# Opening stage of a fused attention, rational MLP and PReLU MLP kernel: zero products ahead of the first scores, two-bank scores, other staging of the loads, and earlier places for three readers of finished accumulators

## The chip, the cores and the metric

One core of one Trainium2 chip. The metric is the device time of one execution in microseconds. The kernel before took 1590.13 us (median of 3 runs, 1588.19 to 1590.34).

## What is computed

Three layers in a row on 2 sequences of 3008 rows, all in float32:

```python
scores = (1/3008) * z @ z.T                 # z: 2 x 3008 x 64
x = u * (maximum(scores, 0)**2 @ v)         # u, v: 2 x 3008 x 256
h = x @ w_in                                # 256 -> 2048
P = a0 + a1*h + a2*h**2 + a3*h**3
Q = 1 + |b0|*|h| + |b1|*h**2
x = (P / (Q + 1e-6)) @ w_out                # 2048 -> 256
h = x @ w_in2                               # 256 -> 2048
out = (maximum(h, 0) + alpha*minimum(h, 0)) @ w_out2
```

The weights of both MLPs are float64 and reach the chip as pairs of 32-bit words; the kernel decodes them itself.

## The kernel before, in words

**Tiling.** The rows are cut into 12 blocks (b, j) of 512 (the last of a sequence has 448). A product of float32 operands is made of float32r products of high and low parts, so a block has 190 attention matmuls (48 of scores, 142 of values), 192 of the first MLP and 192 of the second: 574, and 6888 for the 12 blocks, each of 128x128 by 512 columns (or 448).

**Attention.** `a_stream` walks the blocks; a step takes one pair of key tiles, kp of 12. `a_scores` makes two score tiles with two matmuls each (L266, L267), from zA and zB, which hold high and low parts of z. Relu by ScalarE (L268, one for each of the two tiles), then Square (L269), then `split` into ahi (L91 on ScalarE; for block (0, 0) L93 on VectorE) and alo (L94 on VectorE). `a_values` adds the step's product with vt three steps later (LAG_A) to the accumulator acca (L297, L306). After the last step `a_end` multiplies acca by u (L336, tile ut) and stores the block to DRAM. There is one accumulator acca, shared in PSUM (tag acc0) with the second MLP's acc2; acc1 has the first MLP's.

**Opening.** The first HEAD=30 attention steps run alone. Beside them the sixteen pieces of the first MLP's weights are loaded (`words`, L148, on SyncE's queue), decoded (`decode`: L133, L136, L139, L141, L142, L143 on VectorE and L134 on ScalarE) and split (L93, L94 on VectorE). `weights_due` says how many pieces are due by a step: RD0=0.62 per step. In the first 12 steps z (L213, L218, L225) and v (L100, L91, L93, L94) of the first sequence are loaded and split as well. All these loads, and ut, share the two buffers of the tag "raw" (RAW=2). The tag "big" has 28 buffers: 12 of vt and 16 of weights.

**Then** 40 steps of the first MLP (`m1_hidden`, `m1_back`, 24 matmuls each) are spread over the other 115 attention steps, and the second MLP's weights are decoded and spilled to DRAM (`spill_w`, every fifth step, except steps 64 to 75). Then the rest of the first MLP runs against the second. `m1_end` (L424) and `m2_end` (L462) copy finished accumulators out by ScalarE.

**Order.** Each engine has one queue, in order. A scheduler writes the order before the run: of what is ready by its own clock, what comes first in the program goes first. `tc.high_priority(EARLY)` counts an instruction as 100 places earlier. Constants (the four a, the two b, alpha, and sg and sal made from alpha: L187 to L201) are made at the start.

Of the kernel before, what the change touches and what calls it, by code (L numbers as in the profile page):

```python
# [7 lines left out]
F32 = mybir.dt.float32  # L8
# [12 lines left out]

HEAD, X1 = 30, 40

RD0, RD = 0.62, 0.62

# [4 lines left out]
EARLY = 100  # L30
# [5 lines left out]
def relu2_attention_rational_mlp_prelu_mlp(  # L36
# [47 lines left out]

    def raw_tile(nm):
        return tmp.tile([P, 1024], F32, tag="raw", name=nm, bufs=RAW)


# [23 lines left out]
    def load_v(b, kp):  # L112

        raw = raw_tile("vraw")
        r3 = raw.rearrange("p (c d) -> p c d", c=4)
        r0 = kp * 2 * P
        load_rows(r3, v[b], r0, min(S - r0, 4 * P))
        for i in range(2):
            t = big.tile([P, 2, 2, D], F32R, tag="big", name="vt")
            split(t[:, 0], t[:, 1], r3[:, 2 * i : 2 * i + 2, :], on_act=b > 0 or i % 2 == 0)  # L120
            if kp + i == NKP - 1:

                h2 = t[HALF:P, 0, 1].bitcast(F32)
                nc.vector.tensor_tensor(t[HALF:P, 1, 1], h2, h2, ALU.subtract)
            vt[b, kp + i] = t
# [20 lines left out]
    def words(src):  # L146
        raw = tmp.tile([P, 2, 512], I32, tag="raw", name="wraw", bufs=RAW)
        nc.sync.dma_start(out=raw, in_=src.rearrange("(c p) f -> p c f", p=P))  # L148
        return raw.rearrange("p c (n t) -> p (c n) t", t=2)
# [31 lines left out]
    def fill_w(store, jp):  # L181
        t = late.get("w", big).tile([P, 2, 2, 256], F32R, tag="big", name="w")
        nc.gpsimd.dma_start(out=t.rearrange("p k c d -> p k (c d)"), in_=store[jp])
        store[jp] = t

    sc = const.tile([P, 8], F32, name="sc")
    nc.gpsimd.dma_start(out=sc[:, 0:4], in_=pa[None, :].to_broadcast([P, 4]))  # L187
    nc.gpsimd.dma_start(out=sc[:, 4:6], in_=pb[None, :].to_broadcast([P, 2]))
    cb = const.tile([P, 2], F32, name="cb")
    nc.scalar.activation(cb, sc[:, 4:6], AF.Abs)  # L190
    one = const.tile([P, 1], F32, name="one")
    ONE = 1.0 + 1e-6
    nc.vector.memset(one, ONE)
    al = const.tile([P, NF], F32, name="al")
    nc.gpsimd.dma_start(out=al, in_=alpha.rearrange("(c p) -> p c", p=P))

    sg = const.tile([P, NF], F32, name="sg")
    nc.vector.tensor_scalar(sg, al, 1.0, -2.0, ALU.is_gt, ALU.mult)
    nc.vector.tensor_scalar(sg, sg, 1.0, None, ALU.add)
    sal = const.tile([P, NF], F32, name="sal")  # L200
    nc.vector.tensor_tensor(sal, al, sg, ALU.mult)  # L201
    a0, a1, a2, a3 = (sc[:, i : i + 1] for i in range(4))
# [6 lines left out]
    def load_z(b, g):  # L209

        raw = raw_tile("zraw")
        n = qn[g]
        nc.sync.dma_start(out=raw[:, 0:n], in_=zt[b, :, g * QB : g * QB + n])  # L213
        if n % P:
            nc.sync.dma_start(out=raw[:, n : n + HALF], in_=zt[b, :, S - HALF : S])
            n += HALF
        t = zp.tile([P, QB], F32R, tag="z", name="zA")
        nc.vector.tensor_copy(t[:, 0:n], raw[:, 0:n])  # L218
        if (b, g) == (0, 0):
            zB[b, g] = zp.tile([P, QB], F32R, tag="z", name="zB")  # L220
            nc.scalar.copy(zB[b, g][HALF:P, 0:n], raw[HALF:P, 0:n])
            nc.vector.tensor_tensor(
                zB[b, g][0:HALF, 0:n], raw[0:HALF, 0:n], t[0:HALF, 0:n].bitcast(F32), ALU.subtract
            )
        nc.vector.tensor_tensor(  # L225
            t[HALF:P, 0:n], raw[HALF:P, 0:n], t[HALF:P, 0:n].bitcast(F32), ALU.subtract
        )
        zA[b, g] = t
# [24 lines left out]
    def a_scores(b, j, kp):  # L253
        n = qn[j]
        r = tmp.tile([P, 2, QB], F32, tag="t", name="r", bufs=TT)
        pair = None
        if not x1 and kp % 2:
            pair = psw.tile([P, 2, QB], F32, tag="h", name="sp")
        for i in range(2):
# [7 lines left out]
            nc.tensor.matmul(s, w, zB[b, j][:, :n], start=False, stop=True)  # L267
            nc.scalar.activation(r[:, i, :n], s, AF.Relu, scale=1.0 / S)  # L268
        nc.scalar.activation(r[:, :, :n], r[:, :, :n], AF.Square)  # L269
        hi = hlp.tile([P, 2, QB], F32R, tag="hl", name="ahi")  # L270
        lo = hlp.tile([P, 2, QB], F32R, tag="hl", name="alo")
        on_act = (b, j) != (0, 0)
        if kp < NKP - 1:
            split(hi[:, :, :n], lo[:, :, :n], r[:, :, :n], on_act)
        else:

            if on_act:
                nc.scalar.copy(hi[:, :, :n], r[:, :, :n])
            else:
                nc.vector.tensor_copy(hi[:, :, :n], r[:, :, :n])  # L280
            for dst, rows, i in ((lo, slice(0, P), 0), (hi, slice(HALF, P), 1)):
# [51 lines left out]
    def a_end(b, j):  # L333
        n = qn[j]
        t = uts.pop((b, j))
        nc.vector.tensor_tensor(t[:, :, :n], acc_a[b, j][:, :, :n], t[:, :, :n], ALU.mult)  # L336
        xd[b, j] = dr.tile([P, ND, QB], F32, name=f"xd{b}_{j}")
# [80 lines left out]
    def m1_end(q):  # L418
# [4 lines left out]
        t = tmp.tile([P, ND, QB], F32, tag="raw", name="x2", bufs=RAW)  # L423
        nc.scalar.copy(t[:, :, :n], acc1[q][:, :, :n])  # L424
        x2d[q] = dr.tile([P, ND, QB], F32, name=f"x2d{q[0]}_{q[1]}")
# [32 lines left out]
    def m2_end(q):  # L458
        b, j = q
        n = qn[j]  # L460
        t = tmp.tile([P, ND, QB], F32, tag="raw", name="ot", bufs=RAW)
        nc.scalar.copy(t[:, :, :n], acc2[q][:, :, :n])  # L462
        r0 = b * S + j * QB
# [156 lines left out]
```

## Time and profile before

| | |
|---|---|
| median of 3 runs | 1590.13 us |
| profiled execution, its own time | 1588.01 us |
| its span, first to last instruction | 1586.2 us |
| TensorE matmul | 1555.5 us busy, 6888 instructions |
| VectorE (DVE) | 1405.0 us busy, 1505 instructions |
| ScalarE (ACT) | 1183.9 us busy, 1473 instructions |
| GpSimd (POOL) | 28.1 us busy, 55 instructions |
| mean granted clock of TensorE | 0.998 |

A busy time is the union of the spans in which an engine has an instruction in flight; matmuls overlap, so a matmul's own duration (0.39 us) is longer than the distance to the next one, and the distance is what a matmul costs. The same holds for VectorE and ScalarE in a lesser degree. x counts the instructions that touch a stretch, so one that is cut by its edge counts on both sides. The name in brackets behind an instruction of the timeline is how long its engine had been idle before it, and what ended that. PE is TensorE, PEld its weight load, SPq and POOLq the queues of SyncE and GpSimd.

### The profile page before, as it was taken

What the parts mean: (1) busy time and instruction counts of PE and PEld (TensorE: products, weight loads), DVE (VectorE), ACT (ScalarE), POOL (GpSimd) and SP (SyncE); (2) the same over time, 40 slices, a digit from 0 to 9 for tenths busy, and PEclk for the clock granted to TensorE, in tenths of its full rate; (3) what the DMA queues carried; (4) which work ended last, traced back from release to release, by engine and by line L of the source; (5) the groups of instructions that cost most, each with busy time, mean ns of one, the idle gap of its engine ahead of it and who ended that gap; (6) DMA issues with size and microseconds to landing.
All of it is one profiled execution on the core that took longest, in us unless ns stands there. A gap on an engine that the chain in (4) does not pass through costs nothing.

```text
span 1586.2 us, 18045 instructions
## 1 busy us (share of the span) xinstructions
PE 1555.5 (98%) x6888; PEld 1288.9 (81%) x6888; DVE 1405.0 (89%) x1505; ACT 1183.9 (75%) x1473; POOL 28.1 (2%) x55
## 2 busy tenths in 40 slices
PE   7799999999999999999999999999999999999998
PEld 5587788788888888888888888888888888888888
DVE  7998989999899899877999989899899999898963
ACT  5598899989988899988576666676666666676643
POOL 0000000000000000001000000000000000000000
PEclk9999999999999999999999999999999999999999
DMA  4433211233212121104301000100101000000000
GB/s 126 132 100 120 61 52 54 80 97 93 61 53 87 42 84 41 58 34 149 127 1 40 26 27 1 41 27 25 41 0 39 14 27 35 17 14 27 14 1 25
DMA packets 39911, 83.03 MB, mean 52 GB/s; under 512 B 3600, under 2 KB 12816, under 8 KB 39824
## 3 DMA queue, kind: packets, MB, share of 16 engines
q1 hardware_dynamic: 32800, 65.09, 12.8%
q0 software_dynamic: 7024, 16.79, 3.4%
q8 instruction: 54, 0.88, 0.2%
q14 instruction: 33, 0.27, 0.1%
HBM read 52.64 MB, written 26.41 MB: 50 GB/s over the span
## 4 chain that ended last, share of the span: by engine, by line
PE 89%; DVE 5%; ACT 3%; DMA 1%; issue 1%; POOL 0%; DVEq 0%; SPq 0%; ACTq 0%; POOLq 0%
PE acc L297 21%; PE acca L297 13%; PE h L288 11%; PE h L289 10%; PE acc L306 10%; PE h L290 10%; PE acca L306 6%; PE s L266 3%; PE s L267 3%; DVE alo L94 1%; ACT r L269 1%; ACT r L268 1%; ACT ahi L91 0%; DMA zraw<-in_z_dram 0%; DVE ahi L93 0%
## 5 line engine op out<-in xcount | busy, mean ns | idle before, releaser
L297 PE MATMUL acc<-ghi,w 128*128 128x512 f32 (+1 forms) x1536 | 377.7, 385 | 0.0
L297 PEld LDWEIGHTS acc<-ghi,w 128*128 128x128 f32 x1536 | 288.2, 188 | 54.0 <-ACT ghi L91 0.2
L297 PE MATMUL acca<-ahi,vt 128*128 128x512 f32 (+1 forms) x1152 | 292.6, 389 | 7.5 <-DVE ut L336 5.5
L288 PE MATMUL h<-xhi,w 128*128 128x512 f32 (+1 forms) x768 | 296.5, 387 | 0.1
L289 PE MATMUL h<-xlo,w 128*128 128x512 f32 (+1 forms) x768 | 296.2, 386 | 0.0
L290 PE MATMUL h<-xhi,w 128*128 128x512 f32 (+1 forms) x768 | 296.0, 386 | 0.0
L297 PEld LDWEIGHTS acca<-ahi,vt 128*128 128x128 f32 x1152 | 216.8, 189 | 53.1 <-DVE ut L336 6.7
L392 ACT ACTIVATE sq<-h 128x1024 f32<-128x1024 f32 (+1 forms) x96 | 97.3, 1013 | 154.2 <-PE h L290 147.9
L443 ACT ACTIVATE m<-h,sal 128x512 f32<-128x512 f32 (+1 forms) x192 | 127.8, 680 | 106.7 <-PE h L290 106.1
L306 PE MATMUL acc<-glo,w 128*128 128x512 f32 (+1 forms) x768 | 203.5, 385 | 0.3 <-DVE glo L409 0.3
L94 DVE TENSOR_TENSOR alo<-r,ahi 128x1024 fp32r<-128x1024 f32 (+1 forms) x132 | 158.1, 1199 | 36.0 <-PE acc L297 18.5
L288 PEld LDWEIGHTS h<-xhi,w 128*128 128x128 f32 x768 | 144.2, 188 | 30.5 <-DVE m L444 0.9
L94 DVE TENSOR_TENSOR glo<-m,ghi 128x1024 fp32r<-128x1024 f32 (+1 forms) x96 | 115.2, 1200 | 58.7 <-PE acc L297 41.9
L289 PEld LDWEIGHTS h<-xlo,w 128*128 128x128 f32 x768 | 144.2, 188 | 27.4 <-DVE xlo L94 0.7
L306 PEld LDWEIGHTS acc<-glo,w 128*128 128x128 f32 x768 | 144.1, 188 | 27.5 <-DVE glo L409 0.7
L290 PEld LDWEIGHTS h<-xhi,w 128*128 128x128 f32 x768 | 144.2, 188 | 26.9
L268 ACT ACTIVATE r<-s 128x512 f32<-128x512 f32 (+1 forms) x256 | 143.6, 598 | 26.2 <-DVE t L408 20.3
L306 PE MATMUL acca<-alo,vt 128*128 128x512 f32 (+1 forms) x552 | 150.6, 389 | 2.6 <-DVE alo L94 2.6
L444 DVE SCALAR_TENSOR_TENSOR m<-h,sg,m 128x512 f32<-128x512 f32 (+1 forms) x192 | 138.6, 736 | 16.2 <-ACT m L443 15.5
L269 ACT ACTIVATE r<-r 128x1024 f32<-128x1024 f32 (+1 forms) x144 | 151.8, 1058 | 1.6
L396 DVE SCALAR_TENSOR_TENSOR ab<-sq,cb,ab 128x1024 f32<-128x1024 f32 (+1 forms) x96 | 120.7, 1258 | 14.3 <-ACT ab L393 14.1
L406 DVE SCALAR_TENSOR_TENSOR ghi<-t,sc,sq 128x1024 fp32r<-128x1024 f32 (+1 forms) x96 | 120.9, 1259 | 10.8 <-ACT sq L402 5.6
(70 smaller groups left out, 2083.1 us busy)
## 6 DMA issues: line engine op xcount, KB each, us to landing
wraw<-in_moe_w_in_dram SPq DMA_DIRECT2D x16, 512.0 KB, 3.7
wraw<-in_moe_w_out_dram SPq DMA_DIRECT2D x16, 512.0 KB, 3.6
wd<-dec POOLq DMA_DIRECT2D x32, 256.0 KB, 2.3
w<-wd POOLq DMA_DIRECT2D x16, 512.0 KB, 4.2
vraw<-in_v_dram SPq DMA_DIRECT2D x10, 512.0 KB, 3.8
ut<-in_u_dram SPq DMA_DIRECT2D x10, 512.0 KB, 3.7
xd<-ut SPq DMA_DIRECT2D x10, 512.0 KB, 2.6
xr<-xd SPq DMA_DIRECT2D x10, 512.0 KB, 3.3
```

Of the source, the lines that this page charges most:

```text
L94: nc.vector.tensor_tensor(dst_lo, src, dst_hi.bitcast(F32), ALU.subtract)
L268: nc.scalar.activation(r[:, i, :n], s, AF.Relu, scale=1.0 / S)
L269: nc.scalar.activation(r[:, :, :n], r[:, :, :n], AF.Square)
L288: nc.tensor.matmul(acc, w_hi, hi, start=first, stop=False)
L289: nc.tensor.matmul(acc, w_hi, lo, start=False, stop=False)
L290: nc.tensor.matmul(acc, w_lo, hi, start=False, stop=last)
L297: nc.tensor.matmul(acc[:, e, :n], w[:, k, i, e * P : (e + 1) * P], hi[:, i, :n], start=first and i == 0 and k == 0, stop=False,)
L306: nc.tensor.matmul(acc[:, e, :n], w[:, 0, i, e * P : (e + 1) * P], lo[:, i, :n], start=False, stop=last and i == both - 1,)
L396: nc.vector.scalar_tensor_tensor(ab, sq, b1, ab, ALU.mult, ALU.add)
L406: nc.vector.scalar_tensor_tensor(hi, t, a0, sq, ALU.add, ALU.mult)
L443: nc.scalar.activation(t[:, i], h, AF.Copy, scale=sal[:, f : f + 1])
L444: nc.vector.scalar_tensor_tensor(t[:, i], h, sg[:, f : f + 1], t[:, i], ALU.mult, ALU.max)
```

## The change

The first 36 attention steps run alone (30 before), with RD0 0.4 and RD 0.55 pieces of weights per step. Nine matmuls of a zeroed tile (WARM) stand ahead of everything. In the opening the scores of a step lie in two neighbouring banks, in turn of tag h and of the still unused acc1, and one Relu reads both. Block (0, 0) splits on ScalarE like the others. The first sequence's z and v are staged in buffers of the tag "big". The weight words come by GpSimd's queue. Constants are made on GpSimd, with alpha laid out by the host, loaded first. zA's low part is made ahead of zB. The readers of finished accumulators count as 100 places earlier.

```diff
@@ -19,9 +19,11 @@
 
 LAG_A, LAG_M = 3, 2
 
-HEAD, X1 = 30, 40
-
-RD0, RD = 0.62, 0.62
+HEAD, X1 = 36, 40
+
+RD0, RD = 0.4, 0.55
+
+WARM = 9
 
 SP, AV0, AV1 = 5, 64, 76
 
@@ -82,8 +84,18 @@
     zp = zctx.enter_context(tc.tile_pool(name="zp", bufs=ZP))
     late = {}
 
-    def raw_tile(nm):
+    def raw_tile(nm, early=False):
+
+        if early:
+            return big.tile([P, 1024], F32, tag="big", name=nm)
         return tmp.tile([P, 1024], F32, tag="raw", name=nm, bufs=RAW)
+
+
+    wz = hlp.tile([P, QB], F32R, tag="hl", name="wz")
+    nc.vector.memset(wz.bitcast(F32), 0.0)
+    wps = psw.tile([P, QB], F32, tag="s", bufs=2, name="wps")
+    for i in range(WARM):
+        nc.tensor.matmul(wps, wz[:, 0:P], wz, start=i == 0, stop=i == WARM - 1)
 
 
     def split(dst_hi, dst_lo, src, on_act=True):
@@ -111,7 +123,7 @@
 
     def load_v(b, kp):
 
-        raw = raw_tile("vraw")
+        raw = raw_tile("vraw", b == 0)
         r3 = raw.rearrange("p (c d) -> p c d", c=4)
         r0 = kp * 2 * P
         load_rows(r3, v[b], r0, min(S - r0, 4 * P))
@@ -145,7 +157,7 @@
 
     def words(src):
         raw = tmp.tile([P, 2, 512], I32, tag="raw", name="wraw", bufs=RAW)
-        nc.sync.dma_start(out=raw, in_=src.rearrange("(c p) f -> p c f", p=P))
+        nc.gpsimd.dma_start(out=raw, in_=src.rearrange("(c p) f -> p c f", p=P))
         return raw.rearrange("p c (n t) -> p (c n) t", t=2)
 
     def raw_w(src, jp, wide):
@@ -183,22 +195,26 @@
         nc.gpsimd.dma_start(out=t.rearrange("p k c d -> p k (c d)"), in_=store[jp])
         store[jp] = t
 
+    al = const.tile([P, NF], F32, name="al")
+    nc.gpsimd.dma_start(out=al, in_=alpha)
     sc = const.tile([P, 8], F32, name="sc")
     nc.gpsimd.dma_start(out=sc[:, 0:4], in_=pa[None, :].to_broadcast([P, 4]))
     nc.gpsimd.dma_start(out=sc[:, 4:6], in_=pb[None, :].to_broadcast([P, 2]))
     cb = const.tile([P, 2], F32, name="cb")
-    nc.scalar.activation(cb, sc[:, 4:6], AF.Abs)
     one = const.tile([P, 1], F32, name="one")
     ONE = 1.0 + 1e-6
     nc.vector.memset(one, ONE)
-    al = const.tile([P, NF], F32, name="al")
-    nc.gpsimd.dma_start(out=al, in_=alpha.rearrange("(c p) -> p c", p=P))
 
     sg = const.tile([P, NF], F32, name="sg")
-    nc.vector.tensor_scalar(sg, al, 1.0, -2.0, ALU.is_gt, ALU.mult)
-    nc.vector.tensor_scalar(sg, sg, 1.0, None, ALU.add)
     sal = const.tile([P, NF], F32, name="sal")
-    nc.vector.tensor_tensor(sal, al, sg, ALU.mult)
+
+    nc.gpsimd.tensor_scalar(sg, al, 1.0, -2.0, ALU.is_gt, ALU.mult)
+    nc.gpsimd.tensor_scalar(sg, sg, 1.0, None, ALU.add)
+    nc.gpsimd.tensor_tensor(sal, al, sg, ALU.mult)
+    nc.gpsimd.tensor_scalar(cb, sc[:, 4:6], 0.0, 2.0, ALU.is_ge, ALU.mult)
+    nc.gpsimd.tensor_scalar(cb, cb, -1.0, None, ALU.add)
+    nc.gpsimd.tensor_tensor(cb, sc[:, 4:6], cb, ALU.mult)
+
     a0, a1, a2, a3 = (sc[:, i : i + 1] for i in range(4))
     b0, b1 = cb[:, 0:1], cb[:, 1:2]
 
@@ -208,7 +224,7 @@
 
     def load_z(b, g):
 
-        raw = raw_tile("zraw")
+        raw = raw_tile("zraw", b == 0)
         n = qn[g]
         nc.sync.dma_start(out=raw[:, 0:n], in_=zt[b, :, g * QB : g * QB + n])
         if n % P:
@@ -216,15 +232,15 @@
             n += HALF
         t = zp.tile([P, QB], F32R, tag="z", name="zA")
         nc.vector.tensor_copy(t[:, 0:n], raw[:, 0:n])
+        nc.vector.tensor_tensor(
+            t[HALF:P, 0:n], raw[HALF:P, 0:n], t[HALF:P, 0:n].bitcast(F32), ALU.subtract
+        )
         if (b, g) == (0, 0):
             zB[b, g] = zp.tile([P, QB], F32R, tag="z", name="zB")
             nc.scalar.copy(zB[b, g][HALF:P, 0:n], raw[HALF:P, 0:n])
             nc.vector.tensor_tensor(
                 zB[b, g][0:HALF, 0:n], raw[0:HALF, 0:n], t[0:HALF, 0:n].bitcast(F32), ALU.subtract
             )
-        nc.vector.tensor_tensor(
-            t[HALF:P, 0:n], raw[HALF:P, 0:n], t[HALF:P, 0:n].bitcast(F32), ALU.subtract
-        )
         zA[b, g] = t
 
 
@@ -253,9 +269,13 @@
     def a_scores(b, j, kp):
         n = qn[j]
         r = tmp.tile([P, 2, QB], F32, tag="t", name="r", bufs=TT)
+
         pair = None
-        if not x1 and kp % 2:
-            pair = psw.tile([P, 2, QB], F32, tag="h", name="sp")
+        if not x1:
+            if kp % 2:
+                pair = psw.tile([P, 2, QB], F32, tag="h", name="sp")
+            else:
+                pair = psa.tile([P, 2, QB], F32, tag="acc1", name="sq")
         for i in range(2):
             k = 2 * kp + i
             w = zA[b, k // 4][:, (k % 4) * P : (k % 4 + 1) * P]
@@ -265,19 +285,18 @@
                 s = psw.tile([P, QB], F32, tag="s", bufs=2, name="s")[:, :n]
             nc.tensor.matmul(s, w, zA[b, j][:, :n], start=True, stop=False)
             nc.tensor.matmul(s, w, zB[b, j][:, :n], start=False, stop=True)
-            nc.scalar.activation(r[:, i, :n], s, AF.Relu, scale=1.0 / S)
+            if pair is None:
+                nc.scalar.activation(r[:, i, :n], s, AF.Relu, scale=1.0 / S)
+        if pair is not None:
+            nc.scalar.activation(r[:, :, :n], pair[:, :, :n], AF.Relu, scale=1.0 / S)
         nc.scalar.activation(r[:, :, :n], r[:, :, :n], AF.Square)
         hi = hlp.tile([P, 2, QB], F32R, tag="hl", name="ahi")
         lo = hlp.tile([P, 2, QB], F32R, tag="hl", name="alo")
-        on_act = (b, j) != (0, 0)
         if kp < NKP - 1:
-            split(hi[:, :, :n], lo[:, :, :n], r[:, :, :n], on_act)
+            split(hi[:, :, :n], lo[:, :, :n], r[:, :, :n])
         else:
 
-            if on_act:
-                nc.scalar.copy(hi[:, :, :n], r[:, :, :n])
-            else:
-                nc.vector.tensor_copy(hi[:, :, :n], r[:, :, :n])
+            nc.scalar.copy(hi[:, :, :n], r[:, :, :n])
             for dst, rows, i in ((lo, slice(0, P), 0), (hi, slice(HALF, P), 1)):
                 nc.vector.tensor_tensor(
                     dst[rows, i, :n], r[rows, i, :n], hi[rows, i, :n].bitcast(F32), ALU.subtract
@@ -333,7 +352,8 @@
     def a_end(b, j):
         n = qn[j]
         t = uts.pop((b, j))
-        nc.vector.tensor_tensor(t[:, :, :n], acc_a[b, j][:, :, :n], t[:, :, :n], ALU.mult)
+        with tc.high_priority(EARLY):
+            nc.vector.tensor_tensor(t[:, :, :n], acc_a[b, j][:, :, :n], t[:, :, :n], ALU.mult)
         xd[b, j] = dr.tile([P, ND, QB], F32, name=f"xd{b}_{j}")
         nc.sync.dma_start(out=xd[b, j][:, :, :n], in_=t[:, :, :n])
 
@@ -421,7 +441,8 @@
             x2[q] = split_x(acc1[q], n)
             return
         t = tmp.tile([P, ND, QB], F32, tag="raw", name="x2", bufs=RAW)
-        nc.scalar.copy(t[:, :, :n], acc1[q][:, :, :n])
+        with tc.high_priority(EARLY):
+            nc.scalar.copy(t[:, :, :n], acc1[q][:, :, :n])
         x2d[q] = dr.tile([P, ND, QB], F32, name=f"x2d{q[0]}_{q[1]}")
         nc.sync.dma_start(out=x2d[q][:, :, :n], in_=t[:, :, :n])
 
@@ -459,7 +480,8 @@
         b, j = q
         n = qn[j]
         t = tmp.tile([P, ND, QB], F32, tag="raw", name="ot", bufs=RAW)
-        nc.scalar.copy(t[:, :, :n], acc2[q][:, :, :n])
+        with tc.high_priority(EARLY):
+            nc.scalar.copy(t[:, :, :n], acc2[q][:, :, :n])
         r0 = b * S + j * QB
         nc.sync.dma_start(
             out=out[:, r0 : r0 + n].rearrange("(e p) s -> p e s", p=P), in_=t[:, :, :n]
@@ -602,6 +624,8 @@
             a = a.transpose(0, 2, 1)
         if name == "z":
             a = _np.concatenate([a, a], axis=2).transpose(0, 2, 1)
+        if name == "moe2_alpha":
+            a = a.reshape(-1, 128).T
         a = _np.ascontiguousarray(a)
         if a.dtype == _np.float64:
             a = a.view(_np.int64)
```

## Rows read from the trace of the kernel before

**Rows 1.** The page: busy times, and tenths of each of 40 slices.
```profile
PE 1555.5 (98%) x6888; PEld 1288.9 (81%) x6888; DVE 1405.0 (89%) x1505; ACT 1183.9 (75%) x1473; POOL 28.1 (2%) x55
...
PE   7799999999999999999999999999999999999998
```

**Rows 2.** Windows: PE, PEld, DVE, ACT, POOL busy (x), granted clock, DMA share, GB/s.
```profile
0.00:160.00 160.00, 136.22 (x547) 104.34 (x548) 140.11 (x228) 112.44 (x160) 3.67 (x9) 0.98 0.40 119
40.00:80.00 40.00, 29.92 (x108) 20.70 (x107) 37.88 (x64) 22.55 (x33) 0.00 (x0) 0.92 0.46 132
80.00:120.00 40.00, 40.00 (x174) 32.30 (x173) 37.36 (x66) 36.56 (x51) 0.00 (x0) 0.99 0.33 99
120.00:160.00 40.00, 36.65 (x158) 28.52 (x157) 34.92 (x52) 32.97 (x45) 1.10 (x2) 1.00 0.38 118
160.00:300.00 140.00, 140.00 (x613) 113.53 (x612) 128.20 (x136) 128.12 (x162) 5.32 (x10) 1.00 0.19 59
```

**Rows 3.** Chain that ended last, one steady step of 24 matmuls: start, us, what.
```profile
1058.76 1.81 PE acc L297 x8
...
1064.20 1.81 PE acc L297 x8
```

**Rows 4.** Timeline, the start on VectorE and TensorE: start, us, engine, line.
```profile
0.81 0.06 DVE L193 MEMSET one<- 128x1 f32 x1 [0.81 <-PEq L597]
3.51 0.43 DVE L218 CAST zA<-zraw 128x512 fp32r<-128x512 f32 x1 [2.65 <-DMA zraw<-in_z_dram]
7.45 0.17 DVE L198 TENSOR_SCALAR sg<-al 128x16 f32<-128x16 f32 x1 [2.79 <-DMA al<-in_moe_alpha_dram]
7.66 0.69 DVE L225 TENSOR_TENSOR zA<-zraw,zA 64x512 fp32r<-64x512 f32 x1
8.40 0.80 PE L266 MATMUL s<-zA 128*128 128x512 f32 x1 [8.40 <-DVE zA L225]
...
15.00 1.26 PE L297 MATMUL acca<-ahi,vt 128*128 128x512 f32 x3
16.10 0.40 PE L266 MATMUL sp<-zA 128*128 128x512 f32 x1
```

**Rows 5.** Waits of TensorE over the span: us in total, times, longest.
```profile
PE s L266 <- DVE zA L225: 9.3, 2, 8.4
PE acca L297 <- DVE ut L336: 5.5, 2, 3.2
```

**Rows 6.** Waits of ScalarE, 0 to 150 us.
```profile
ACT dec L134 <- DVE dec L133: 24.5, 7, 4.9
```

**Rows 7.** Timeline of VectorE, 45 to 48 us: the distances between starts.
```profile
45.53 0.68 DVE L143 TENSOR_TENSOR dec<-dec 128x512 f32<-128x512 f32 x1
46.13 1.22 DVE L94 TENSOR_TENSOR alo<-r,ahi 128x1024 fp32r<-128x1024 f32 x1
47.27 0.42 DVE L93 CAST w<-dec 128x512 fp32r<-128x512 f32 x1
47.61 0.42 DVE L133 TENSOR_SCALAR dec<-wraw 128x512 f32<-128x512 f32 x1
```

**Rows 8.** Timeline of ScalarE: Relu, Square and ahi, two each without idle time.
```profile
21.16 1.08 ACT L268 ACTIVATE r<-s 128x512 f32<-128x512 f32 x2
72.24 2.01 ACT L269 ACTIVATE r<-r 128x1024 f32<-128x1024 f32 x2
74.14 2.00 ACT L91 CAST ahi<-r 128x1024 fp32r<-128x1024 f32 x2
```

**Rows 9.** The page: a two-bank read of PSUM by ScalarE.
```profile
L392 ACT ACTIVATE sq<-h 128x1024 f32<-128x1024 f32 (+1 forms) x96 | 97.3, 1013 | 154.2 <-PE h L290 147.9
```

**Rows 10.** The page: DMA issues, KB each, median us to landing.
```profile
wraw<-in_moe_w_in_dram SPq DMA_DIRECT2D x16, 512.0 KB, 3.7
...
w<-wd POOLq DMA_DIRECT2D x16, 512.0 KB, 4.2
```

**Rows 11.** The instructions of line L288: ns min/median/max, first and last start.
```profile
L288 PE MATMUL h<-xhi,w x768: 362/389/501, 145.4 to 1573.3; 128*128 128x512 f32 x160, 128*128 128x448 f32 x32
```

## The prediction

> **What bounds the kernel now.** I read the page first. TensorE is busy in nearly every slice [rows 1], so the question is where it issues more slowly than it can. A steady first-MLP step shows the pace: 24 matmuls in 1064.20 - 1058.76 = 5.44 us, so 0.2267 us each [rows 3]. The windows are then read by their matmul counts, not by their busy times. Up to 160 us there are 547 matmuls; at that pace they need 124.0 us, so **36.0 us are lost in the opening**. From 160 to 300 us 613 matmuls need 139.0 of 140 us: behind the opening little is lost [rows 2]. Of the 36.0 us, 8.4 go before the first matmul [rows 4]. 40 to 80 us holds 108 matmuls where 176 would fit, some 15.5 us lost; 80 to 120 us holds 174 and loses next to nothing; 120 to 160 us holds 158 and loses 4 [rows 2].
>
> Next, why. VectorE is busy for 37.88 of the 40 us from 40 to 80 us, and ScalarE for only 22.55 [rows 2]: VectorE is the bound there; the granted clock is 0.92, as TensorE waits. ScalarE stood still behind it, 24.5 us at the second step of the weight decode [rows 6]. TensorE's waits name the rest: 9.3 us for zA, of which 8.4 are the start, and 5.5 us for the product with u, which sits in the same VectorE queue [rows 5]. At the start zA's second half (L225) runs at 7.66 us although z was there at 3.51 us, because sg (L198), ahead of it in the queue, waited for alpha [rows 4].
>
> **The needs of the opening, in us, before and after.** Distances between starts are what an instruction costs: on VectorE 0.60 for L143, 1.14 for alo, 0.34 for a 512-wide cast [rows 7]. One piece of weights is three passes like L133 and one cast (0.34 each) and four like L143 (0.60): 3.76. Ahi on VectorE is taken as 0.60 too.
>
> - VectorE, 30 steps before: alo 30 x 1.14 = 34.2; ahi of block (0, 0) 12 x 0.60 = 7.2; 16 pieces 60.2; v, twelve low parts and seven casts, 9.6; z 6.2; u 2.3. Sum 119.7. TensorE needs 30 x 15.83 x 0.2267 = 107.7. VectorE is 12.0 over.
> - VectorE, 36 steps after: alo 41.0; ahi moves to ScalarE; 60.2; 9.6; 6.2; u 3.4. Sum 120.4, against 36 x 15.83 x 0.2267 = 129.2 on TensorE: 93%. Up to step 12, where z and v are still being split, 4 pieces in place of 6 make it 44.5 against 43.1, so it is no longer far behind there either.
> - ScalarE after: one two-bank Relu, bounded by half of L269's pair (1.0) and by a two-bank read of PSUM, 1.01 [rows 8, 9]; with Square 1.0 and ahi 1.0 [rows 8] that is 3.0 per step, 108 for 36; v casts and decode passes, 22 at about 0.54 (half of L268's pair), 12. Sum 120: 93%. The two single Relus cost 1.08 before, so merging saves 0.07 a step and no more; the move of ahi adds 12 x 1.0.
>
> So the six extra steps and the slower weights give TensorE more to do while VectorE's pile is worked off, and no engine is over-booked. **What the opening then loses:**
>
> 1. The start. The memset of the zero tile costs between 0.06 (a 128x1 memset) [rows 4] and 0.42 (a cast of its size) [rows 7] behind 0.81 us. Nine matmuls at the start's spacing follow. Before, 15 matmuls ran from 8.40 to 16.10 us with one wait of about 1 us in them; I take 0.43 each, which is the lower of the clock's two levels, 1.2 GHz for 512 columns. They end at 4.8 to 5.1 us. The constants now wait on POOL, so zA is complete at about 3.51 + 0.34 + 0.60, with some latency 4.7. First real matmul at **5.1** in place of 8.4.
> 2. The clock. Those 15 matmuls lost 15 x 0.2 = 3.0 us; spacing came down at 16.10, 7.7 us after TensorE's first matmul [rows 4]. The nine zero products take 3.8 of that. Between nothing and 1.9 us remains: **1.0**. That zero products raise the clock is shown by no row; if they don't, it is the 3.0 again.
> 3. Filling. Scores, Relu, Square, ahi come one after another, about 4 us, before the first values; steps 2 and 3 need the second z. Twelve early loads no longer wait for two buffers (12 loads, 12 vt and the 4 pieces of weights due by step 12 are just the 28 buffers of "big"), but they share the wires. 0 to 4; I take **2.0**.
> 4. The rest of some 125 us. Like 160 to 300 us, with both engines at about 92%, it would lose 0.7%, 0.9 us; like 120 to 160 us 10%, 12.5. Loads by engine put it near the first, the uneven decode work near the second: **7.0**.
>
> Together 15.1 in place of 36.0: **20.9 gained**. The 5.5 us of the waits for u are inside the 36.0 and not counted again; an earlier place helps only the product that is ready. No wait of TensorE names the two ScalarE copies L424 and L462, so their new places gain nothing; each moves one 1.0 us instruction past its neighbours, cost nothing while ScalarE has a tenth of its time free (128.12 of 140 us) [rows 2].
>
> **Given back.** 40 first-MLP steps go on 109 attention steps, not 115: 0.367 per step for 0.348. With seven two-bank VectorE passes of 1.14 or more, that adds 0.15 us to VectorE's 5.02 (128.20/140 of 5.48) [rows 2] while the step grows to 5.59: 93% for 92%. The spills begin ten steps later and end at step 130, five before the fills. 0 to 3 us; I take **1.5**.
>
> The weight words pass from SP's queue to POOL's. On POOL the median from issue to landing is 4.2 us for such a size, on SP 3.7 [rows 10]. 0.5 us each is hidden by two buffers and a decode every 1.8 to 2.5 steps (6 us or more); were it not, 16 x 0.5 = 8 us would fill VectorE's slack of 8.8 in the opening and no more. Between 0 and 8 I take 0. Behind a late load stands all of VectorE's work behind L133. On SP's queue the loads of z, v and u stand behind 16 issues fewer in the opening; on POOL's, the spills' stores come only after step 40. The Trainium skill speaks against this move ("SBUF — State Buffer", section "SBUF: two separate sides"): descriptors of POOL's loads can't be written while VectorE holds the shared port in certain passes, and the load then seems blocked by VectorE; the SP queue is free of that. By [rows 10] the sum stays as it is; by that rule it would be the third rival below.
>
> **Sum:** 1588.0 (the profiled execution: span 1586.2 and 1.8 around it) - 20.9 + 1.5 = 1568.6. The median of the runs is 2.1 above the profiled execution; I go between and say **1570**.
>
> **Rivals.**
>
> - *All of it comes in* (0.15). Items 2 and 3 at nothing, item 4 as from 160 to 300 us: 5.1 + 0.9 lost, 30 gained, 1.5 given back: 1559.5. For it: nothing is over-booked. Against: a static order written for other durations.
> - *ScalarE takes VectorE's place* (0.20). It now has ahi, and stays in order behind decodes: with the 24.5 us of [rows 6] unchanged its need is 144.5 against 129.2, 15 in place of the 7 of item 4; with the 5.5 for u as well the loss is 28.9, the gain 7.1 - 1.5: 1582. For it: 93% booked. Against: the wait follows VectorE's lateness, which shrinks.
> - *Late weight words* (0.05). If each load holds VectorE at L133 for 1.5 us, three times the difference of [rows 10], that is 16 x 1.5 = 24 us, less the slack of 8.8: 15 more, 1585. It decides from 8.8/16 = 0.55 us per load. Against: each load has a whole decode's time to land.
> - *The middle jams*, **slower** (0.07). Place: attention beside the first MLP, about 600 us. Price: where VectorE was 95% booked and late, TensorE lost 15.5 of 40 us [rows 2]. It decides from 100% of 5.59 us on VectorE; 93% is reckoned. If a tenth of that stretch fell into it, 60 x 0.39 = 23 us more: 1592. Against: 80 to 120 us was at 93% and lost nothing.
> - *The change doesn't do what it says* in one part, the zero products: 2 us, within the forecast's own range.
>
> The forecast itself has 0.53, its own range 1563 to 1577. A measurement of this kernel can tell 0.2%, 3.2 us, from no change. Faster takes the forecast, the first rival, and most of the next two, 0.88; same 0.05, slower 0.07. The range reaches over most of the first rival and into the second: 1559 to 1582.
>
> **What would show it.** First score matmul near 5 us, at 0.23 us spacing before 10; 40 to 80 us with 160 matmuls or more; VectorE and ScalarE both near 93% there; no wait for ut above 1 us; ScalarE's wait for L133 well under 24.5; the first h matmul of the first MLP at 142 to 150 us, where it was (145.4) [rows 11], yet six steps further; windows behind 300 us as before. Wrong: under 150 matmuls from 40 to 80 us, VectorE waiting for weight words, or matmul counts behind 160 us down by more than 1%.

## The result, and the profile after

The changed kernel takes **1570.13 us** (median of 4 runs, 1568.46 to 1571.51) against 1590.18 us for the kernel before (here 4 runs, where the prediction had 3): a ratio of 0.9876, 95% interval 0.9859 to 0.9893. That is 20.0 us less. The forecast was 1570, with a range from 1559 to 1582.

The page of the changed kernel, busy times and TensorE's slices:

```profile
PE 1551.7 (99%) x6897; PEld 1291.1 (82%) x6897; DVE 1399.4 (89%) x1491; ACT 1191.8 (76%) x1445; POOL 54.2 (3%) x93
...
PE   8999999999999999999999999999999999999998
```

The windows answer to [rows 2]; columns as there:

```profile
0.00:160.00 160.00, 150.80 (x636) 121.42 (x637) 138.03 (x212) 133.59 (x151) 18.23 (x31) 0.99 0.39 120
...
40.00:80.00 40.00, 38.77 (x169) 31.09 (x168) 35.96 (x56) 34.36 (x40) 3.03 (x5) 1.00 0.33 99
80.00:120.00 40.00, 38.21 (x161) 31.09 (x161) 37.20 (x61) 33.48 (x38) 4.33 (x6) 0.96 0.37 110
120.00:160.00 40.00, 38.53 (x168) 31.11 (x167) 33.48 (x47) 34.98 (x39) 2.89 (x4) 1.00 0.32 101
160.00:300.00 140.00, 140.00 (x619) 114.72 (x619) 131.26 (x140) 127.22 (x163) 7.60 (x13) 1.00 0.20 63
```

Up to 160 us TensorE now issues 636 matmuls, 9 of them the zero products. The other 627 need 142.1 us at 0.2267 us each, so the opening loses 17.9 us where it lost 36.0. Call that **the loss in the opening**, and what is left of the span without it **the rest**: 1567.8 - 17.9 = 1549.9 us, against 1586.2 - 36.0 = 1550.2 before. In the profiled executions, whose spans differ by 18.4 us, the gain thus lies in the first 160 us but for 0.3 us. 40 to 80 us has 169 matmuls where it had 108; VectorE is at 90% there, no longer at 95%, and ScalarE at 86% in place of 56%.

The start, on the timeline of VectorE and then of TensorE, answers to [rows 4]:

```profile
0.90 0.48 DVE L95 MEMSET wz<- 128x512 f32 x1 [0.90 <-PEq L619]
3.56 0.43 DVE L234 CAST zA<-zraw 128x512 fp32r<-128x512 f32 x1 [2.17 <-DMA zraw<-in_z_dram]
4.02 0.69 DVE L235 TENSOR_TENSOR zA<-zraw,zA 64x512 fp32r<-64x512 f32 x1
8.94 0.43 DVE L234 CAST zA<-zraw 128x512 fp32r<-128x512 f32 x1 [1.85 <-DMA zraw<-in_z_dram]
1.44 4.21 PE L98 MATMUL wps<-wz 128*128 128x512 f32 x9 [1.44 <-DVE one L206]
5.44 0.63 PE L286 MATMUL sq<-zA 128*128 128x512 f32 x1
5.87 0.63 PE L286 MATMUL sp<-zA 128*128 128x512 f32 x1
6.30 0.44 PE L287 MATMUL sq<-zB,zA 128*128 128x512 f32 x1
10.24 0.47 PE L286 MATMUL sq<-zA 128*128 128x512 f32 x1 [2.35 <-ACT r L292]
...
13.04 2.14 PE L316 MATMUL acca<-ahi,vt 128*128 128x512 f32 x8 [0.74 <-ACT ahi L103]
```

The zero products start at 1.44 us and end as the first real one begins, at 5.44 us. Two more matmuls come at 0.43 us, then the spacing is down to 0.23. TensorE then stops for 2.35 us, to 10.24. What holds it is the second z: VectorE can use it only from 8.94 us, and its low part, made from 9.40 us on, ends at 10.09. The row names a Square (L292), which ends at the same time and gives the scores nothing; in no_zero, below, the same stop is named after zA.

The waits, of TensorE over the span and of ScalarE to 150 us, answer to [rows 5, 6], and the DMA issues to [rows 10]:

```profile
PE acca L316 <- DVE ut L356: 2.2, 2, 1.8
...
ACT dec L146 <- DVE dec L145: 10.0, 3, 6.3
...
wraw<-in_moe_w_in_dram POOLq DMA_DIRECT2D x16, 512.0 KB, 4.2
```

The first matmul of the first MLP (L307) starts at 148.6 us, six attention steps further than at 145.4 [rows 11].

### The profile page after: what moved, and what is told of

It is laid out like the page before. It is cut to its first block, busy times and chain, and to the rows that moved or that the text cites. A ratio compares the mean times of both kernels' runs of the same rounds, so it can differ in the third digit from the quotient of the medians.

```text
span 1567.8 us, 18040 instructions
## 1 busy us (share of the span) xinstructions
PE 1551.7 (99%) x6897; PEld 1291.1 (82%) x6897; DVE 1399.4 (89%) x1491; ACT 1191.8 (76%) x1445; POOL 54.2 (3%) x93
## 4 chain that ended last, share of the span: by engine, by line
PE 89%; DVE 6%; ACT 3%; DMA 1%; issue 1%; SPq 0%; DVEq 0%; ACTq 0%; POOLq 0%
PE acc L316 21%; PE acca L316 13%; PE acc L325 10%; PE h L307 10%; PE h L308 10%; PE h L309 10%; PE acca L325 6%; PE s L286 3%; PE s L287 3%; DVE alo L106 1%; DMA vraw<-in_v_dram 1%; ACT r L292 0%; DVE ghi L426 0%; PE sq L286 0%; PE sq L287 0%
## 5 line engine op out<-in xcount | busy, mean ns | idle before, releaser
L307 PE MATMUL h<-xhi,w 128*128 128x512 f32 (+1 forms) x768 | 296.3, 386 | 0.0
L307 PEld LDWEIGHTS h<-xhi,w 128*128 128x128 f32 x768 | 144.2, 188 | 29.5 <-issue 1.2
L292 ACT ACTIVATE r<-r 128x1024 f32<-128x1024 f32 (+1 forms) x144 | 150.5, 1052 | 1.7
L103 ACT CAST ahi<-r 128x1024 fp32r<-128x1024 f32 (+1 forms) x132 | 135.7, 1033 | 1.1 <-PE acc L325 0.8
L289 ACT ACTIVATE r<-s 128x512 f32<-128x512 f32 (+1 forms) x210 | 115.7, 590 | 21.7 <-DVE t L428 21.7
```

The lines of the kernel that those rows point to most:

```text
L103: nc.scalar.copy(dst_hi, src)
L307: nc.tensor.matmul(acc, w_hi, hi, start=first, stop=False)
```

## The experiments

All but one start from the changed kernel and undo or move one part. The table puts the median beside the loss in the opening (160 us less 0.2267 us for each matmul up to there, zero products taken off) and the rest, both of the profiled execution. The 95% interval of a ratio to the kernel before reaches about 0.0015, 2.4 us, to either side, so differences of some 3 us and less in the table can't be told from none.

| kernel | median us | against changed | loss in the opening | rest |
|---|---|---|---|---|
| before | 1590.18 | +20.0 | 36.0 | 1550.2 |
| changed | 1570.13 | | 17.9 | 1549.9 |
| only_pace | 1578.99 | +8.9 | 26.9 | 1550.6 |
| old_pace | 1584.72 | +14.6 | 34.4 | 1548.9 |
| rd_old | 1579.36 | +9.2 | 25.8 | 1551.6 |
| head42 | 1575.80 | +5.7 | 15.8 | 1558.8 |
| old_readers | 1575.84 | +5.7 | 17.2 | 1556.4 |
| copies_own | 1566.25 | -3.9 | 18.3 | 1548.8 |
| no_zero | 1573.62 | +3.5 | 19.4 | 1552.1 |
| split_dve | 1571.65 | +1.5 | 20.1 | 1549.7 |
| old_staging | 1569.89 | -0.2 | 18.1 | 1549.8 |
| old_banks | 1569.46 | -0.7 | 17.4 | 1549.4 |
| words_sp | 1568.46 | -1.7 | 17.4 | 1548.8 |
| lean | 1568.09 | -2.0 | 17.9 | 1548.5 |

**old_pace: the old pace alone undone.**

```diff
-HEAD, X1 = 36, 40
-RD0, RD = 0.4, 0.55
+HEAD, X1 = 30, 40
+RD0, RD = 0.62, 0.62
```

> The changed kernel with the old pace: 30 steps alone, 0.62 pieces of weights per step; all else as changed. Theory A (the opening was over-booked on VectorE, and the new pace is the largest single term): VectorE needs 112.5 us for 30 steps, TensorE 107.7, so 4.8 us over, plus some 3 us of queueing: 8 us slower than the changed kernel, 1578, and 40 to 80 us with about 150 matmuls. Theory B (the start, the staging and the split of block (0, 0) bring the gain, the pace little): 1571 to 1573.

Measured: 1584.72 us (9 runs), a ratio to before of 0.9975, interval 0.9965 to 0.9985. Nearly three quarters of the gain are gone, more than theory A gave. The window from 40 to 80 us, then its timeline on VectorE, TensorE and ScalarE:

```profile
40.00:80.00 40.00, 33.21 (x122) 25.26 (x121) 34.65 (x58) 25.18 (x30) 3.62 (x5) 0.87 0.35 107
```

```profile
47.92 0.69 DVE L154 SCALAR_TENSOR_TENSOR dec<-wraw,dec 128x512 f32<-128x512 uint32 x1
48.53 0.42 DVE L234 CAST zA<-zraw 128x512 fp32r<-128x512 f32 x1
48.87 0.68 DVE L155 TENSOR_TENSOR dec<-dec 128x512 f32<-128x512 f32 x1
49.58 0.69 DVE L235 TENSOR_TENSOR zA<-zraw,zA 64x512 fp32r<-64x512 f32 x1
...
57.71 1.23 DVE L106 TENSOR_TENSOR alo<-r,ahi 128x1024 fp32r<-128x1024 f32 x1 [3.93 <-ACT ahi L103]
...
50.41 0.47 PE L286 MATMUL sq<-zA 128*128 128x512 f32 x1 [3.06 <-DVE zA L235]
...
52.12 1.02 ACT L291 ACTIVATE r<-sq 128x1024 f32<-128x1024 f32 x1 [5.65 <-PE sq L287]
```

The trace shows how an over-booked VectorE costs more than the sum says. Decode instructions stand ahead of a z in VectorE's queue. TensorE waits 3.06 us for it, ScalarE 5.65 us for TensorE's scores, and then VectorE itself 3.93 us for ScalarE's ahi. VectorE is at 87% in this stretch, below the 90% of the changed kernel, and yet 47 matmuls fewer are issued: one late instruction in an in-order queue came back to its own engine as idle time. After its wait TensorE issued two matmuls 0.31 us apart and the next seven 0.43; the granted clock is 0.56 from 50.4 to 54 us, 0.87 over the 40 us.

**only_pace: the pace alone, in the kernel before.**

```diff
-HEAD, X1 = 30, 40
-RD0, RD = 0.62, 0.62
+HEAD, X1 = 36, 40
+RD0, RD = 0.4, 0.55
```

> The kernel before with nothing changed but the pace: 36 steps alone, 0.4 and 0.55 pieces per step. Theory A: VectorE needs 127.6 us (ahi of block (0, 0) still on it) against TensorE's 129.2, so the 12 us over are gone but it is 99% booked, and the start (8.4 us, slow clock) stays: 1580, 10 us faster than before. Theory B: 1587 to 1590.

Measured: 1578.99 us beside 1589.23 for before in the same runs, 10.2 us less, as theory A had it (ratio 0.9937, interval 0.9920 to 0.9953). **Half of the gain is these two lines.** The first matmul is still at 8.50 us, and 40 to 80 us holds 136 matmuls. The parts do not simply add up: the pace is worth 10.2 us in the kernel before and 14.6 in the changed one, and all the other parts together 4.5 without it (1589.23 to 1584.72). The 9.0 us by which the opening of the changed kernel is better still are divided by the runs below only in part.

**rd_old: 36 steps alone, the old rate of weights.**

```diff
-RD0, RD = 0.4, 0.55
+RD0, RD = 0.62, 0.62
```

> The changed kernel with 36 steps alone, but the weights at the old 0.62 pieces per step. Theory G (it is the rate of decoding: VectorE needs 110 us in the first 28 steps against TensorE's 100.5, and what is lost there isn't regained in the eight light steps after): 1578 to 1583, 40 to 80 us with 125 to 145 matmuls, as in old_pace (122). Theory H (it is the later start of the first MLP, whose steps no longer meet unfinished weights): 1570 to 1573, and 120 to 160 us with about 168 matmuls, where old_pace has 131.

Measured: 1579.36 us. Windows:

```profile
40.00:80.00 40.00, 33.61 (x142) 25.70 (x141) 35.89 (x62) 26.81 (x32) 3.61 (x5) 1.00 0.36 111
...
120.00:160.00 40.00, 37.88 (x160) 30.84 (x160) 26.30 (x35) 35.87 (x39) 1.04 (x2) 0.96 0.23 69
```

Theory G is borne out: the rate of decoding alone costs 9.2 of the 14.6 us. 40 to 80 us holds 27 matmuls fewer than in the changed kernel, 6.1 us, and what is lost there does not come back, though VectorE stands at only 66% from 120 to 160 us. By difference the later start of the first MLP brings the other 5.4: 160 matmuls from 120 to 160 us, where old_pace has 131.

**head42: further in the same direction.**

```diff
-HEAD, X1 = 36, 40
-RD0, RD = 0.4, 0.55
+HEAD, X1 = 42, 40
+RD0, RD = 0.4, 0.43
```

> The changed kernel with 42 steps alone and 0.4 and 0.43 pieces per step. Theory A (VectorE's need per step decides): 128 us against 151, the opening loses 3 to 6 us less, up to 2 us given back in the middle: 1565 to 1569. Rival (the opening's remaining loss is the start and single stops, not the booking): 1569 to 1573.

Measured: 1575.80 us, slower than the changed kernel, outside both expectations. Windows of head42, then of the changed kernel, then two instructions of head42:

```profile
280.00:360.00 80.00, 74.39 (x324) 60.83 (x323) 71.62 (x76) 67.11 (x91) 1.26 (x2) 0.98 0.36 107
360.00:640.00 280.00, 279.80 (x1221) 226.98 (x1220) 260.24 (x268) 253.16 (x317) 16.32 (x27) 1.00 0.19 60
```

```profile
280.00:360.00 80.00, 79.66 (x365) 67.73 (x364) 77.42 (x85) 73.53 (x99) 1.79 (x3) 1.00 0.37 114
360.00:640.00 280.00, 278.69 (x1218) 226.24 (x1217) 256.52 (x266) 251.35 (x316) 16.31 (x27) 1.00 0.19 60
```

```profile
298.44 1.14 ACT L103 CAST vt<-vraw 128x512 fp32r<-128x512 f32 x2 [3.79 <-DMA vraw<-in_v_dram]
305.04 0.48 PE L286 MATMUL s<-zA 128*128 128x448 f32 x1 [2.08 <-ACT r L289]
```

The opening gets 2.1 us better, as wanted, but the rest gets 8.9 us worse. Nearly all of that lies between 280 and 360 us: 41 matmuls fewer than in the changed kernel, and none fewer from there to 640 us. This is the place of the prediction's rival that ends slower, the middle that jams, but not its cause: VectorE is at 90% in that stretch, where the changed kernel, which loses nothing there, has it at 97%. The longest stop there is ScalarE's, 3.79 us for a load of v; then come casts of v and the first MLP's instructions in its queue, and TensorE waits 2.08 us for a Relu behind them. That the late load starts the loss is read from this order and was not tested.

**old_readers and copies_own: the readers at their own places, all three or the two copies only.**

```diff
-        with tc.high_priority(EARLY):
-            nc.vector.tensor_tensor(t[:, :, :n], acc_a[b, j][:, :, :n], t[:, :, :n], ALU.mult)
+        nc.vector.tensor_tensor(t[:, :, :n], acc_a[b, j][:, :, :n], t[:, :, :n], ALU.mult)
...
-        with tc.high_priority(EARLY):
-            nc.scalar.copy(t[:, :, :n], acc1[q][:, :, :n])
+        nc.scalar.copy(t[:, :, :n], acc1[q][:, :, :n])
...
-        with tc.high_priority(EARLY):
-            nc.scalar.copy(t[:, :, :n], acc2[q][:, :, :n])
+        nc.scalar.copy(t[:, :, :n], acc2[q][:, :, :n])
```

(copies_own has the last two only.)

> The changed kernel with the three readers (product with u, two copies) at their own places in the order. Theory A (they gain nothing apart from the wait for u in the opening, now 2.2 us): between 1570 and 1573, the waits of TensorE for ut from 2.2 to at most 5.5 us, none for the copies. Theory D (the earlier places carry a real part of the gain): 1575 or more.

> The changed kernel with only the product with u at its earlier place, the two copies of finished accumulators at their own. Theory A for the copies (no wait of TensorE names them): 1570, within 1.5 us of the changed kernel; the 5.7 us of old_readers then belong to the product alone. Rival: 1573 or more.

Measured: 1575.84 us for old_readers, 1566.25 for copies_own. The product with u is worth more than was thought, and the copies nothing. In old_readers the opening is as good as in the changed kernel; the loss is behind it. Timeline of VectorE and TensorE, 287 to 296 us:

```profile
287.33 1.09 DVE L106 TENSOR_TENSOR alo<-r,ahi 128x896 fp32r<-128x896 f32 x1
288.33 0.42 DVE L105 CAST dec<-dec 128x512 fp32r<-128x512 f32 x1
288.67 0.42 DVE L234 CAST zA<-zraw 128x512 fp32r<-128x512 f32 x1
289.00 0.69 DVE L106 TENSOR_TENSOR dec<-dec 128x512 fp32r<-128x512 f32 x1
289.72 0.69 DVE L235 TENSOR_TENSOR zA<-zraw,zA 64x512 fp32r<-64x512 f32 x1
290.44 1.23 DVE L355 TENSOR_TENSOR ut<-acca,ut 128x1024 f32<-128x1024 f32 x1
...
288.11 0.37 PE L287 MATMUL s<-zB,zA 128*128 128x448 f32 x1
291.81 3.21 PE L316 MATMUL acca<-ahi,vt 128*128 128x448 f32 x8 [3.33 <-DVE ut L355]
294.86 0.97 PE L325 MATMUL acca<-alo,vt 128*128 128x448 f32 x4
```

The product stands behind alo, two decode instructions and two for z, none of which TensorE needs as soon. It waits 3.33 us, and then issues eight matmuls in 3.05 us, 0.38 each, at a granted clock of 0.52; the next eight of this kind, from 295.67 us, take 1.62 us, 0.2025 each. That is 1.4 us more, and the stretch from 160 to 300 us ends with 590 matmuls where the changed kernel has 619. In the kernel before no such wait stands in this stretch. Nor does one in only_pace, which has the new pace and the product at its own place: TensorE waits for it once, 2.0 us, in the opening, and the rest is 1550.6 us. So it is not the pace by itself that puts the product behind the others, but the order that the scheduler writes for the changed kernel as a whole; which part of the change does it was not tested. The earlier place takes the product out again. With all three readers in place of one, the changed kernel is slower than copies_own by 3.9 us on the medians, but the intervals of the ratios overlap (0.9859 to 0.9893 and 0.9837 to 0.9866), and the traces show no one wait for it; it stays open.

**no_zero: without the zero products.**

```diff
-    wz = hlp.tile([P, QB], F32R, tag="hl", name="wz")
-    nc.vector.memset(wz.bitcast(F32), 0.0)
-    wps = psw.tile([P, QB], F32, tag="s", bufs=2, name="wps")
-    for i in range(WARM):
-        nc.tensor.matmul(wps, wz[:, 0:P], wz, start=i == 0, stop=i == WARM - 1)
```

> The changed kernel without the nine zero products and their tile. Theory A (the clock term is 2 us of its own): first real matmul at 4.7 us, about 15 matmuls at 0.43 us spacing, some 2 us slower: 1572. Theory C (what the clock gives is lost again, as TensorE then waits for ScalarE and the second z): same as changed, 1570, with the same time of the first value product (13.0 us).

Measured: 1573.62 us, 3.5 us more. Its timeline of TensorE:

```profile
4.75 0.80 PE L279 MATMUL sq<-zA 128*128 128x512 f32 x1 [4.75 <-DVE zA L228]
...
9.89 0.47 PE L279 MATMUL sq<-zA 128*128 128x512 f32 x1 [1.35 <-DVE zA L228]
...
12.98 2.14 PE L309 MATMUL acca<-ahi,vt 128*128 128x512 f32 x8 [1.01 <-ACT ahi L96]
```

The first eight matmuls come 0.43 us apart from 4.75 us on, then TensorE waits for the second z in either kernel, and the first values start at 12.98 us, with the zero products at 13.04. Theory C holds for the start: the pace that they bring forward is not on the path there. The median is above both expectations all the same. By the traces the 3.5 us lie later: 157 matmuls from 40 to 80 us where the changed kernel has 169, with one wait of 2.1 us for ScalarE's ahi, and 2.2 us in the rest. The interval of the ratio, 0.9885 to 0.9915, just overlaps that of the changed kernel. Whether the zero products, another order of the queues or chance makes the difference is not shown.

**split_dve: ahi of block (0, 0) on VectorE.**

```diff
-            split(hi[:, :, :n], lo[:, :, :n], r[:, :, :n])
+            split(hi[:, :, :n], lo[:, :, :n], r[:, :, :n], (b, j) != (0, 0))
```

> The changed kernel with ahi of block (0, 0) on VectorE again (L93's kind in place of ScalarE's). Theory A (VectorE is the tighter engine in the first 12 steps: 44.5 + 7.2 us against 43.1): 1573 to 1576. Theory F (ScalarE is the tighter one now): 1568 or less.

Measured: 1571.65 us, 1.5 us more, which the scatter of the runs could make, and between the two expectations; the opening loses 2.2 us more. From 40 to 80 us TensorE has one long wait, 2.8 us, for an ahi that VectorE makes (L105). The sign is theory A's, the size below it.

**old_staging, words_sp, old_banks, and lean: three parts that brought nothing.**

```diff
-        raw = raw_tile("vraw", b == 0)
+        raw = raw_tile("vraw")
...
-        raw = raw_tile("zraw", b == 0)
+        raw = raw_tile("zraw")
```

> The changed kernel with z and v of the first sequence staged in the two buffers of tag raw again, beside the weight words and u. Theory A: the loads of z and v start only when a buffer is free, the filling grows by about 4 us: 1574, with waits for z or v on VectorE above 6 us up to 150 us. Theory B (staging is a main term): 1580 or more.

```diff
-        nc.gpsimd.dma_start(out=raw, in_=src.rearrange("(c p) f -> p c f", p=P))
+        nc.sync.dma_start(out=raw, in_=src.rearrange("(c p) f -> p c f", p=P))
```

> The changed kernel with the weight words on SyncE's queue again. Theory A (the queue doesn't matter, the landing of 4.2 in place of 3.7 us is hidden): 1570, within 2 us. Theory E (POOL's queue makes words late: VectorE's 1.9 us of waits for wraw in the opening, and the 6.3 us stop of ScalarE behind one of them, come from it): 1566 to 1568.

```diff
-        if not x1:
-            if kp % 2:
-                pair = psw.tile([P, 2, QB], F32, tag="h", name="sp")
-            else:
-                pair = psa.tile([P, 2, QB], F32, tag="acc1", name="sq")
+        if not x1 and kp % 2:
+            pair = psw.tile([P, 2, QB], F32, tag="h", name="sp")
...
-            if pair is None:
-                nc.scalar.activation(r[:, i, :n], s, AF.Relu, scale=1.0 / S)
-        if pair is not None:
-            nc.scalar.activation(r[:, :, :n], pair[:, :, :n], AF.Relu, scale=1.0 / S)
+            nc.scalar.activation(r[:, i, :n], s, AF.Relu, scale=1.0 / S)
```

> The changed kernel with the scores of the opening in two single banks and one pair again, and a Relu for each bank. Theory A (merging saves ScalarE 0.07 us a step, 2.5 us in all, not on the path): 1570 to 1572. Theory F (ScalarE is the bound of the opening now, and the freeing of both banks at once matters): 1574 or more.

lean has all three of these edits at once.

> The changed kernel with three parts undone together that alone showed no loss when undone: words on SyncE's queue, z and v in the two buffers of tag raw, single banks in the opening. If they are each without effect: 1568 to 1571. If one covered for another (with all three undone z, v, u and the words share two buffers and one queue as before): 1574 or more, with waits of VectorE for z and v in the opening above 6 us.

Measured: 1569.89, 1568.46, 1569.46 and 1568.09 us. None is slower than the changed kernel, nor are the three together; their intervals overlap with its own. For old_staging that is outside both expectations: VectorE does wait longer for z and v up to 150 us, 10.0 us where the changed kernel has 5.3, but no time is lost by it. In words_sp VectorE's waits for words, 1.9 us, are gone and ScalarE's for the decode fall from 10.0 to 5.5 us; that too is worth nothing beyond the scatter. old_banks refutes theory F, and lean is as expected if each part is without effect. The timeline of words_sp, queue of SyncE, VectorE and TensorE, shows what the loads do to one another:

```profile
1.64 0.50 SPq L160 DMA_DIRECT2D wraw<-in_moe_w_in_dram  x1
...
2.18 0.47 SPq L160 DMA_DIRECT2D wraw<-in_moe_w_out_dram  x1
...
2.70 0.47 SPq L229 DMA_DIRECT2D zraw<-in_z_dram  x1
...
12.85 0.43 DVE L234 CAST zA<-zraw 128x512 fp32r<-128x512 f32 x1 [5.67 <-DMA zraw<-in_z_dram]
...
14.15 0.76 PE L286 MATMUL sq<-zA 128*128 128x512 f32 x1 [5.77 <-DVE zA L235]
```

Two loads of words go ahead of the second z, which lands some 4 us later than in the changed kernel. In lean z, v and words share two buffers, and the shortage keeps the words back: the first load of words goes out at 21.77 us. The first 20 us hold 64 matmuls, more than in any other kernel here. First the changed kernel, then lean:

```profile
0.00:20.00 20.00, 15.47 (x55) 11.99 (x56) 13.49 (x23) 14.93 (x18) 6.60 (x15) 1.00 0.89 279
```

```profile
0.00:20.00 20.00, 16.50 (x64) 12.76 (x65) 13.20 (x23) 16.06 (x23) 3.82 (x13) 1.00 0.46 132
```

The changed kernel moves 279 GB/s in that time, lean 132. words_sp has 36 matmuls in these 20 us, and yet by 160 us it has lost 17.4 us, lean and the changed kernel 17.9 each: what is lost or won at the very start is made good before the opening ends.

## Why the prediction was right, point by point

- **The booking.** 36.0 us were lost, 15.1 were forecast to remain, 17.9 did. VectorE and ScalarE stand at 90% and 86% from 40 to 80 us, where both were forecast near 93%. That the pace at which VectorE is given its work was the largest cause is shown three ways: old_pace and rd_old lose again from 40 to 80 us, and only_pace gains half of the whole by two lines.
- **Item 1, the start.** 5.1 forecast, 5.44 measured; the zero products begin 0.2 to 0.6 us later than reckoned, as the memset starts at 0.90 us and takes 0.48.
- **Item 2, the clock.** 1.0 forecast. Two matmuls at 0.43 us after 5.44 us cost 0.4. The spacing alone speaks for the lower level of the clock here: the granted clock of the profile reads 1.00 from 1.4 to 6.3 us. But the step around it was wrong: the 3.0 us that the slow start cost before were taken as lost on the path, and no_zero shows that at the start nothing follows from them, as the second z is later.
- **Item 3, the filling.** 2.0 forecast, 2.35 + 0.74 = 3.1 measured. The bounds held. The staging was given as a help here, and old_staging shows none.
- **Item 4.** 7.0 forecast. 17.9 less 5.4, 0.4 and 3.1 leaves 9.0. Of this 3.5 lie from 80 to 120 us, where TensorE waits 1.79 us for the product with u and issues more slowly behind it; the forecast had no wait for ut above 1 us.
- **Adding the items up** was itself a weak step: words_sp issues 19 matmuls fewer than the changed kernel in the first 20 us and has lost no more than it by 160 us, so the start is no term that stands by itself.
- **Given back.** 1.5 forecast, and the rest is 0.3 us shorter than before. The first MLP's denser steps cost nothing that shows; that the term is so small also needs the next one.
- **The readers: the step that failed.** "An earlier place helps only the product that is ready", and counts for nothing outside the 36.0, was argued from the waits of the kernel before. In the changed kernel's order the product would be late at another place, and old_readers, where it is, loses 6.5 us behind the opening. For the copies the step held: without their earlier places nothing is lost.
- **The figure itself** was hit more closely than the reckoning deserves. The opening kept 2.8 us more than forecast, 1.8 us of what was to be given back did not come, and the 1.4 us added on the way from the profiled execution to the median stand against 0.4 measured (1570.13 less 1569.73). That these nearly cancel is luck.
- **ScalarE** was said to take VectorE's place with a chance of 0.20. It is at 86% from 40 to 80 us, its wait for the decode fell from 24.5 to 10.0 us, and old_banks, which gives it more and shorter instructions, loses nothing.
- **The words on POOL's queue.** Medians to landing of 4.2 and 3.8 us against 3.7 and 3.6, and VectorE waits 1.9 us for them in the opening. The Trainium skill ("SBUF — State Buffer", section "SBUF: two separate sides") says that the descriptors of POOL's loads can't be written while VectorE holds the shared port in certain passes, so that the load seems blocked. Here, beside a VectorE at 86% or more, the loads land half a microsecond later at most in the median; words_sp, which has them on SyncE's queue, is 1.7 us faster, within what the runs scatter. Which of VectorE's passes hold the port no run here shows.

The rival of the jammed middle was refused for this change, rightly. In head42 the same stage does get slower, but not by the rival's mechanism. Reckoned as in the prediction, its 40 first-MLP steps on 103 attention steps ask 5.34 us of VectorE in a step of 5.70, 94%, far from the 100% from which the rival was to decide; the loss is a few stops in one stretch of 80 us.

## What to carry to other kernels

Where one engine prepares data for a later stage, spread that work so that the preparing engine has slack in every step of the stage, and not only in the sum; two lines that set this pace were worth half of a change of many parts. Then measure a step further too: head42 shows that more of the same can lose in the next stage. An instruction that frees a single accumulator should go first in its queue, even where the trace shows no wait for it: the next change of order may put it behind others. Undo each part of a joint change alone: the staging, the queue of the words, the two-bank scores and the earlier places of the copies could be undone here without loss. The new place of the constants and the order of z's parts were not undone alone. With them TensorE's first real matmul can start at 4.75 us (no_zero) where only_pace has 8.50, but what that is worth in the total is not shown.

## What the runs showed that was not expected

- **A short wait can cost more than its length.** After 3.33 us without a matmul (old_readers, 288 to 292 us) eight matmuls came 0.38 us apart in place of 0.2025. After 1.79 us in the changed kernel eight of 512 columns took 107.66 - 104.67 = 2.99 us, 0.37 each, at a granted clock of 0.63. First these, then the same place in copies_own and in old_readers:

```profile
104.67 3.20 PE L316 MATMUL acca<-ahi,vt 128*128 128x512 f32 x8 [1.79 <-DVE ut L356]
107.66 1.60 PE L325 MATMUL acca<-alo,vt 128*128 128x512 f32 x4
```

```profile
106.80 2.11 PE L316 MATMUL acca<-ahi,vt 128*128 128x512 f32 x8 [1.66 <-DVE ut L356]
```

```profile
104.97 2.11 PE L316 MATMUL acca<-ahi,vt 128*128 128x512 f32 x8 [1.81 <-DVE ut L355]
```

  After 1.66 and 1.81 us the eight come faster, 1.95 us from the first of them to the next group in copies_own. A wait of this length costs the slower pace in one execution and not in another.
- **The moment at which the spacing falls moves.** With the same nine zero products from 1.44 us on, the spacing fell at 6.30 us in the changed kernel, at 7.54 in copies_own, and with the first real matmul at 5.38 in rd_old. In copies_own it rose again to 0.43 at 11.03 us, after a wait of 1.82 us, with the granted clock at 0.50 from 11.0 to 16 us; in the changed kernel it stayed at 0.23 after a wait of 2.35 us. The profiled execution of copies_own is the slowest of its four, 1568.88 us against 1565.72 to 1566.71.
- **A good start was worth nothing.** The first 20 us hold 36 matmuls in words_sp, 55 in the changed kernel, 60 in old_staging and in old_banks, and 64 in lean, and the medians of these five differ by 2.0 us at most. old_staging and lean hold the words back and move 132 GB/s in that time; old_banks moves 279 and is as good as old_staging, so the shortage of buffers is not by itself what makes the good start.
